# Beacon attention and a maxout FFN in one kernel: pairs 12 and 13 turned by transposing DMAs, and the loop's steps in other places

## The chip, the cores and the metric

The kernel runs on one core of a Trainium2 chip. The metric is the device time of one execution in microseconds; the comparison is between the kernel before and the changed kernel. The core has a matrix engine (PE, with weight loads shown apart as PEld), a vector engine (DVE), a scalar engine (ACT), GpSimd (POOL) and a sync engine (SP), each with its own queue of instructions that run in order. DMA engines move data beside them. PE writes to PSUM, the others read it from there; everything else lives in SBUF.

## The reference

Attention of 64 heads (8 batches of 8) over 576 tokens of width 64, with 16 beacon keys and values per head in front of the causal part; its output, 4608 tokens of width 512, goes through a feed-forward layer with three input matrices and a maximum.

```python
k_all = concatenate([beacon_k, k], axis=2)          # 16 + 576 keys
v_all = concatenate([beacon_v, v], axis=2)
scores = scale * q @ k_all^T                        # beacons seen by all, the rest causal
a = exp(scores - max) / (sum + 1e-09)
x = (a @ v_all) -> (4608, 512)
h = maximum(maximum(x @ w1, x @ w2), x @ w3)        # 512 -> 768
out = h @ w_out                                     # 768 -> 512, float32
```

## The kernel before

**Pairs.** Two heads of a batch are a pair; there are 32 pairs, four to a batch, and two pairs are a quad. For each pair q and k are needed with the 64 columns of both heads on 128 partitions (qT and kT, six buffers of each, used by pair number modulo 6, lines 146 to 152).

**Load, cast, turn.** A pair's q and k come by two loads on SP into a staging tile `st` (eight buffers, `load_pair`, line 192), are cast to bf16 (`cast_piece`, line 252: 96 partitions by 768 elements, one for q and one for k), and are then turned. There are two ways. Pairs below `P_X` are loaded with six neighbouring tokens to a partition (line 202), turned on PE by 12 transposes against the identity (`turn`, line 393, step "pair"), and copied out of PSUM into order by DVE (kT, line 459) and by ACT or DVE (qT, line 448). Pairs from `P_X` on are loaded in token order (line 207) and turned by two transposing DMAs on SP straight from the cast tile into qT and kT (`cross_piece`, line 374, steps "cross" p 0 and "cross" p 1). `P_X` is 14. The 16 beacon columns of kT are copied in by the step "keys" (line 455).

**Scores and masks.** A pair has four groups of score tiles. The step "scores" p g n (line 498) takes a PSUM tile from a ring of three (two named sc, one named wide), puts n spare matmuls of 320 columns on constant data into it (`spare`, line 474), then the scores (line 509), and issues the exponential on ACT (line 524). "score" and "exp" are its two halves apart. "mask" p g engine sets the causal zeros afterwards, on POOL (line 543, affine select) or on DVE (line 541, product with a triangle).

**Values.** When both pairs of a quad are masked, "values" quad half (line 584) multiplies with v (cast by "cast v", line 311) and with ones for the sums; the first half uses the two banks pv0 and pv1, the second a ring tile. "invert" is a logarithm and an exponential on ACT (lines 604 and 606), "multiply" three products on DVE into xT (line 616).

**FFN.** The remaining PE time is filled with units of the feed-forward layer: "ffn 1" with a bank (pv0, pv1, or one half of a ring tile) is one unit, "ffn 2" two units in one ring tile. A unit is four matmuls of 512 columns (line 646), then a cast or a maximum on DVE (lines 654 and 656), or six matmuls (line 682), a copy to y (line 694) and, later, a store (line 720).

**Order.** There is no scheduler: the lists `first_steps` and `loop_steps` are emitted as written, and each engine's queue has its instructions in that order. Where an instruction needs another engine's result it waits, and everything behind it in its queue waits too. "load" n takes the next loads from a fixed list (pairs, v pieces and beacons by batch); with an engine's name, that engine first writes one element of the staging tile, so the engine and not SP waits for the tile to come free. Beside the change stand lines 1034 to 1071 (where pairs 12 to 15 are loaded), and the steps of pairs 8 to 13 (lines 1076 to 1181).

```python
P_X = 14
def cross_piece(p, i):
    src = stage.pop(("pair16", p, i))
    x0 = i * Nb
    nc.sync.dma_start_transpose(
        out=(qTs, kTs)[i][p % NT][:, x0 : x0 + S].rearrange("d (r p) -> d r p", r=QR),
        in_=src.rearrange("p r h d -> p (r h d)"),
    )
```

Of the kernel before, what the change touches and what calls it, by code (L numbers as in the profile page):

```python
# [16 lines left out]
def kernel(  # L17
# [48 lines left out]
    P_X = 14  # L66
# [92 lines left out]
    ring = [(sc_psum, "sc"), (sc_psum, "sc")]  # L159
# [684 lines left out]
    def start_late():  # L844
# [231 lines left out]
        ("scores", 8, 1, 0),  # L1076
# [5 lines left out]
        ("values", 3, 1, "ring"),  # L1082
        ("mask", 8, 1, "pool"),
        ("mask", 8, 0, "pool"),
        ("mask", 8, 2, "pool"),
        ("multiply",),
# [8 lines left out]
        ("scores", 8, 3, 0),  # L1095
        ("scores", 9, 0, 0),
        ("scores", 9, 1, 0),
        ("mask", 8, 3, "pool"),
        ("mask", 9, 0, "pool"),
        ("mask", 9, 1, "pool"),  # L1100
        ("ffn 1", "pv1"),
# [20 lines left out]
        ("ffn 1", "pv1"),  # L1122
# [4 lines left out]
        ("invert",),  # L1127
        ("exp", 10, 2),
        ("values", 4, 1, "ring"),
        ("mask", 10, 1, "pool"),  # L1130
        ("mask", 10, 0, "pool"),
# [4 lines left out]
        ("ffn 2",),  # L1136
        ("ffn 1", "pv0"),
        ("cast", 12, "pool", "pool"),
        ("load", 1),
        ("cast", 14, "pool", "pool"),  # L1140
        ("load", 1),
# [4 lines left out]
        ("mask", 10, 3, "pool"),  # L1146
        ("mask", 11, 0, "pool"),
# [5 lines left out]
        ("cast", 15, "pool", "pool"),  # L1153
        ("load", 1),
# [5 lines left out]
        ("load", 1),  # L1160
# [5 lines left out]
        ("pair", 13, "act"),  # L1166
        ("keys", 13, "act"),
# [7 lines left out]
        ("values", 5, 0, "pv"),  # L1175
        ("invert",),
        ("exp", 12, 2),
# [3 lines left out]
        ("mask", 12, 2, "pool"),  # L1181
        ("multiply",),
        ("invert",),
        ("multiply",),
        ("ffn 2",),
        ("ffn 1", "pv0"),
# [6 lines left out]
        ("keys", 14, "act"),  # L1193
# [4 lines left out]
        ("cross", 16, 0),  # L1198
        ("cross", 16, 1),
        ("cast", 17, "pool", "pool"),  # L1200
        ("cast v", 3, 0),
        ("scores", 13, 2, 0),
        ("scores", 13, 3, 0),
        ("mask", 13, 2, "pool"),
        ("keys", 15, "act"),
        ("mask", 13, 3, "pool"),
        ("ffn 1", "pv0"),
        ("ffn 1", "pv1"),
        ("ffn 1", "pv0"),
        ("cross", 17, 0),  # L1210
        ("cross", 17, 1),
# [5 lines left out]
        ("values", 6, 0, "pv"),  # L1217
        ("invert",),
        ("exp", 14, 2),
        ("values", 6, 1, "ring"),  # L1220
        ("mask", 14, 1, "pool"),
        ("mask", 14, 0, "pool"),
        ("mask", 14, 2, "pool"),
# [3 lines left out]
        ("load", 1),  # L1227
# [3 lines left out]
        ("cast", 18, "pool", "pool"),  # L1231
        ("ffn 1", "pv1"),
        ("scores", 14, 3, 0),
        ("scores", 15, 0, 0),
        ("scores", 15, 1, 0),
        ("mask", 14, 3, "pool"),
        ("keys", 16, "act"),
        ("mask", 15, 0, "pool"),
        ("mask", 15, 1, "pool"),
        ("ffn 1", "pv0"),  # L1240
        ("cross", 18, 0),
        ("load", 1),
        ("cross", 18, 1),
        ("load", 1),
        ("cast", 19, "pool", "pool"),
# [3 lines left out]
        ("mask", 15, 2, "pool"),  # L1249
        ("keys", 17, "act"),  # L1250
# [3 lines left out]
        ("cross", 19, 1),  # L1254
        ("ffn 1", "pv1"),
        ("load", 1),
# [8 lines left out]
        ("mask", 16, 0, "pool"),  # L1265
# [5 lines left out]
        ("cast", 20, "pool", "pool"),  # L1271
# [3 lines left out]
        ("load", 1),  # L1275
        ("scores", 16, 3, 0),
        ("scores", 17, 0, 0),
        ("scores", 17, 1, 0),
        ("mask", 16, 3, "pool"),
        ("keys", 18, "act"),  # L1280
        ("mask", 17, 0, "pool"),
        ("mask", 17, 1, "pool"),
        ("ffn 1", "pv1"),
        ("ffn 1", "pv0"),
        ("cross", 20, 0),
        ("cross", 20, 1),
        ("load", 1),
# [3 lines left out]
        ("cast v", 4, 0),  # L1291
# [12 lines left out]
        ("score", 18, 2),  # L1304
        ("values", 8, 0, "pv"),
        ("invert",),
        ("exp", 18, 2),
        ("values", 8, 1, "ring"),
        ("mask", 18, 1, "pool"),
        ("mask", 18, 0, "pool"),  # L1310
        ("mask", 18, 2, "pool"),
        ("load", 1),
        ("multiply",),
        ("invert",),
        ("multiply",),
        ("ffn 2",),
        ("ffn 2",),
        ("ffn 1", "pv0"),
        ("cast", 22, "pool", "pool"),
        ("ffn 1", "pv1"),  # L1320
        ("scores", 18, 3, 0),
        ("scores", 19, 0, 0),
        ("scores", 19, 1, 0),
        ("mask", 18, 3, "pool"),
        ("keys", 20, "act"),
# [6 lines left out]
        ("cast", 23, "pool", "pool"),  # L1332
        ("store", 1),
        ("load", 1),
# [9 lines left out]
        ("cross", 23, 0),  # L1344
# [3 lines left out]
        ("load", 1),  # L1348
# [6 lines left out]
        ("mask", 20, 1, "pool"),  # L1355
        ("mask", 20, 0, "pool"),
# [5 lines left out]
        ("cast", 24, "pool", "pool"),  # L1362
# [307 lines left out]
```

## Time and profile before

| | us |
|---|---|
| median of 3 runs | 289.59 |
| lowest, highest | 288.01, 289.97 |
| the profiled execution: its own time | 290.2 |
| the profiled execution: span from first to last instruction | 288.4 |
| casts of pairs on POOL, 48 of them, mean | 0.825 |
| transposing DMAs of q, of k: median to landing | 5.1, 3.8 |

The profile is of one execution. Its page gives each engine's busy time, the same in 40 slices of the span with the granted PE clock, the chain of work that ended last, and groups of instructions by source line (L646 is line 646). A timeline row has start, duration, engine, line, operation, output and inputs, the count, and in brackets the idle time before it and what ended that. A windows row has the stretch, its length, and the busy time of PE, PEld, DVE, ACT and POOL with the count of instructions, then PE's clock, the DMA engines' share and GB/s. The loop's steps begin at about 55 us.

### The profile page before, as it was taken

To read this page: it belongs to the slowest core of one execution; us is meant where nothing else is said; L and a number is where in the kernel's file an instruction comes from. 1 tells how busy PE (TensorE), PEld (TensorE's weight loads), DVE (VectorE), ACT (ScalarE), POOL (GpSimd) and SP (SyncE) were. 2 spreads that over 40 slices of the span, in tenths; PEclk is the share of its full clock that TensorE was granted. 3 is DMA by queue.
4 is the path that set the end of the run, shared out by engine and by line. 5 is a ranking of instruction groups with operands and counts; after the bars stand their busy time and mean duration, and the time that the engine had idled before them with its cause. 6 is when DMAs were issued, how large, how long until landed. Compare 5 with 4: busy or idle time off the path is not lost.

```text
span 288.4 us, 8814 instructions
## 1 busy us (share of the span) xinstructions
PE 279.4 (97%) x3702; PEld 160.2 (56%) x3727; DVE 169.6 (59%) x317; ACT 143.9 (50%) x242; POOL 121.6 (42%) x252
## 2 busy tenths in 40 slices
PE   8999999999999999999999999999999999999994
PEld 6666777654645454545456787445544545444442
DVE  2446788756575657464755764666466555373372
ACT  3776676834656564835483268434852552201200
POOL 4463227736486483738366446564623230000000
PEclk9999999999999999999999999999999999999999
DMA  8999999999999979999999999999793003002103
GB/s 155 145 178 202 218 246 168 236 215 205 198 165 160 188 109 127 202 164 194 164 239 192 194 168 213 204 159 181 194 298 152 2 2 148 0 0 102 46 0 147
DMA packets 118231, 45.30 MB, mean 157 GB/s; under 512 B 107312, under 2 KB 112944, under 8 KB 118192
## 3 DMA queue, kind: packets, MB, share of 16 engines
q1 hardware_dynamic: 111984, 39.20, 76.2%
q0 software_dynamic: 5648, 5.21, 12.0%
q8 instruction: 29, 0.48, 0.7%
q10 hardware_dynamic: 560, 0.33, 0.4%
q14 instruction: 10, 0.08, 0.1%
HBM read 35.13 MB, written 9.44 MB: 155 GB/s over the span
## 4 chain that ended last, share of the span: by engine, by line
PE 89%; ACT 3%; DMA 2%; DVE 2%; POOL 1%; issue 1%; POOLq 0%; ACTq 0%
PE pv L646 21%; PE sc L646 15%; PE wide L646 8%; PE pv L682 6%; PE sc L509 6%; PE sc L682 5%; PE pv L584 4%; PE wide L682 4%; PE wide L584 4%; PE sc L584 4%; DMA quad<-in_k_dram 2%; PE wide L509 2%; PE pv L473 2%; ACT at_sb L524 2%; PE sc L665 1%; PE pv L665 1%
## 5 line engine op out<-in xcount | busy, mean ns | idle before, releaser
L524 ACT ACTIVATE at_sb<-sc 128x736 bf16<-128x736 f32 (+5 forms) x95 | 79.4, 868 | 59.6 <-PE sc L509 58.9
L543 POOL TENSOR_SCALAR_AFFINE_SELECT at_sb<-at_sb 128x256 bf16<-128x256 bf16 (+2 forms) x143 | 52.4, 385 | 110.0 <-ACT at_sb L524 101.2
L646 PEld LDWEIGHTS <-w_sb 128*128 128x128 bf16 x648 | 61.1, 98 | 60.7 <-issue 4.9
L646 PE MATMUL pv<-xT,w_sb 128*128 128x512 bf16 (+1 forms) x315 | 65.3, 347 | 0.3
L646 PE MATMUL sc<-xT,w_sb 128*128 128x512 bf16 (+1 forms) x205 | 45.6, 363 | 0.7 <-issue 0.2
L656 DVE TENSOR_TENSOR hT<-hT,pv 128x512 bf16<-128x512 bf16 x48 | 32.4, 686 | 13.2 <-PE pv L646 13.2
L524 ACT ACTIVATE at_sb<-wide 128x736 bf16<-128x736 f32 (+3 forms) x33 | 27.7, 840 | 23.5 <-PE wide L509 23.3
L255 POOL CAST p<-st 96x768 bf16<-96x768 f32 x48 | 38.2, 825 | 0.0
L682 PEld LDWEIGHTS <-hT 128*128 128x128 bf16 x210 | 19.6, 98 | 23.5 <-issue 1.1
L616 DVE TENSOR_TENSOR xT<-pv,recip 128x288 bf16<-128x288 f32 (+2 forms) x48 | 14.2, 351 | 27.1 <-ACT recip L606 27.0
L509 PE MATMUL sc<-qT,kT 64*128 64x288 bf16 (+6 forms) x298 | 28.0, 277 | 1.4 <-DVE kT L443 0.7
L656 DVE TENSOR_TENSOR hT<-hT,sc 128x1024 bf16<-128x1024 bf16 (+1 forms) x19 | 20.8, 1104 | 12.7 <-PE sc L646 12.5
L584 PEld LDWEIGHTS <-v_sb 128*32 128x32 bf16 (+1 forms) x1408 | 24.8, 96 | 2.7 <-issue 1.5
L509 PEld LDWEIGHTS <-kT 64*128 64x128 bf16 x400 | 14.6, 94 | 20.7 <-issue 12.9
L646 PE MATMUL wide<-xT,w_sb 128*128 128x512 bf16 (+1 forms) x110 | 24.5, 364 | 0.1
L682 PE MATMUL pv<-w_out_sb,hT 128*128 128x512 bf16 x83 | 19.9, 380 | 0.1
L311 POOL CAST v_sb<-st 128x1536 bf16<-128x1536 f32 (+2 forms) x21 | 18.4, 898 | 0.0
L654 DVE CAST hT<-pv 128x512 bf16<-128x512 f32 x20 | 13.7, 688 | 5.0 <-PE pv L646 5.0
L682 PE MATMUL sc<-w_out_sb,hT 128*128 128x512 bf16 x68 | 16.4, 380 | 0.2
L665 PEld LDWEIGHTS <-w_sb 128*128 128x128 bf16 x144 | 13.1, 98 | 3.2 <-issue 1.4
L606 ACT ACTIVATE recip<-lnd 128x288 f32<-128x288 f32 x32 | 14.2, 443 | 1.0
L694 DVE COPY y<-pv 128x512 f32<-128x512 f32 x14 | 9.7, 692 | 8.4 <-PE pv L682 8.1
(119 smaller groups left out, 279.8 us busy)
## 6 DMA issues: line engine op xcount, KB each, us to landing
st<-in_q_dram SPq DMA_DIRECT2D x24, 288.0 KB, 5.8
st<-in_k_dram SPq DMA_DIRECT2D x24, 288.0 KB, 6.4
st<-in_v_dram SPq DMA_DIRECT2D x24, 256.0 KB, 5.4
out_dram<-y SPq DMA_DIRECT2D x9, 512.0 KB, 4.6
out_dram<-y SPq DMA_DIRECT2D x17, 256.0 KB, 4.5
w_sb<-in_moe_w_dram POOLq DMA_DIRECT2D x6, 384.0 KB, 8.3
st<-in_v_dram SPq DMA_DIRECT2D x8, 224.0 KB, 4.9
st<-in_v_dram SPq DMA_DIRECT2D x8, 160.0 KB, 5.0
```

The costliest lines, as they stand in the source:

```text
L255: cast(t16.rearrange("p r h d -> p h r d"), st[0:QP, i * NQ2 : (i + 1) * NQ2].rearrange("p (h r d) -> p h r d", h=2, r=QR),)
L311: cast(v_sb[0:n, t:t1].rearrange("p t h d -> p (t h d)"), st[0:n, (t - t_lo) * H * D : (t1 - t_lo) * H * D],)
L509: nc.tensor.matmul(ps[:, e, off : off + q1 - q0], kT[hs, 128 * t : 128 * t + 128], qT[hs, q0:q1], start=True, stop=True, tile_position=(64 ...
L524: nc.scalar.activation(out=both_heads(p, gi), in_=ps[:, :, 0 : g_width(p, gi)], func=AF.Exp, scale=scale)
L543: nc.gpsimd.affine_select(out=view, in_=view, compare_op=ALU.is_ge, fill=0.0, base=x0, pattern=[[0, 2], [1, hi - lo]], channel_multiplier=-1,)
L584: nc.tensor.matmul(ps[bank][32 * j : 32 * j + 32, lo + q0 - qa : lo + qb - qa], lhsT, at_view(PPQ * quad + j // 2, t, j % 2, q0, qb), star ...
L606: nc.scalar.activation(out=recip, in_=lnd, func=AF.Exp, scale=-1.0)
L616: nc.vector.tensor_mul(xT[:, 2 * g + part - 1, c0 + ca : c0 + cb], ps[bank][:, lo : lo + cb - ca], recip[:, ca:cb],)
L646: nc.tensor.matmul(dst[:, o0 : o0 + n], w_in[i][:, ct, 128 * (ft + f) : 128 * (ft + f + 1)], xT[:, ct, x0 : x0 + n], start=(ct == 0), stop ...
L656: nc.vector.tensor_max(h, h, ps)
L665: nc.tensor.matmul(ps[:, f], w_in[i][:, ct, 128 * (ft + f) : 128 * (ft + f + 1)], xT[:, ct, tb * TOKB + lo : tb * TOKB + hi], start=(ct == 0),
L682: nc.tensor.matmul(ps[:, t - tt] if two else ps, hT[:, ft, 128 * t : 128 * (t + 1)], w_out_sb[:, ft, :], start=(ft == 0), stop=(ft == n_ft ...
```

## The change

`P_X` becomes 12: pairs 12 and 13 too are loaded in token order, and their turns on PE ("pair" 12 and 13) are replaced by "cross" 12 and 13. With that the loop's steps are in other places:

- Casts 12 and 13 stand ahead of cast 11; "cross" 12 behind the loads of v for batch 3 and of the beacons, "cross" 13 behind loads 16 and 17.
- Ten spare matmuls are added: scores(8,1) 2, scores(9,0) 2, scores(8,3) 6.
- Some masks go from POOL to DVE, some casts from POOL to DVE (q of 20, 23, 24, 28, k of 31) or ACT (k of 18), some "keys" from ACT to DVE or POOL.
- Several loads get a gate on DVE or POOL, and several loads, crosses and stores move by a few steps.
- In two places an "ffn 2" becomes two "ffn 1" on half ring tiles.

The first steps are the same in both. The diff, cut to what the text below speaks of:

```diff
-    P_X = 14
+    P_X = 12
...
-        ("scores", 8, 1, 0),
+        ("scores", 8, 1, 2),
         ("scores", 8, 0, 0),
...
-        ("cast", 10, "pool", "pool"),
+        ("cast", 10, "pool", "pool"),
+        ("ffn 2",),
+        ("ffn 1", "pv0"),
+        ("load", 1),
+        ("cast", 12, "pool", "pool"),
+        ("load", 1),
+        ("ffn 1", "pv1"),
+        ("ffn 1", "pv0"),
+        ("scores", 9, 0, 2),
         ("scores", 9, 1, 0),
+        ("scores", 8, 3, 6),
+        ("load", 1),
         ("mask", 8, 3, "pool"),
+        ("mask", 9, 1, "dve"),
+        ("ffn 1", "pv1"),
         ("mask", 9, 0, "pool"),
+        ("ffn 1", "pv0"),
+        ("cross", 12, 0),
+        ("cross", 12, 1),
+        ("cast", 13, "pool", "pool"),
+        ("load", 1),
         ("pair", 10, "act"),
-        ("keys", 10, "act"),
+        ("keys", 10, "dve"),
         ("ffn 1", "pv1"),
         ("cast", 11, "pool", "pool"),
-        ("load", 1),
+        ("load", 1, "pool"),
+        ("ffn 2",),
         ("cast v", 2, 0),
...
         ("ffn 1", "pv1"),
+        ("cross", 13, 0),
         ("pair", 11, "act"),
         ("keys", 11, "act"),
         ("ffn 1", "pv0"),
+        ("ffn 1", "pv1"),
+        ("cross", 13, 1),
         ("cast v", 2, 1),
...
-        ("cast", 12, "pool", "pool"),
-        ("load", 1),
         ("cast", 14, "pool", "pool"),
...
-        ("pair", 12, "act"),
-        ("keys", 12, "act"),
...
-        ("cast", 13, "pool", "pool"),
-        ("load", 1),
...
-        ("pair", 13, "act"),
-        ("keys", 13, "act"),
...
         ("score", 14, 2),
         ("values", 6, 0, "pv"),
-        ("invert",),
         ("exp", 14, 2),
+        ("invert",),
...
-        ("cast", 18, "pool", "pool"),
+        ("cast", 18, "pool", "act"),
...
         ("ffn 2",),
-        ("cast", 20, "pool", "pool"),
+        ("load", 1),
+        ("cast", 20, "dve", "pool"),
         ("ffn 1", "pv0"),
         ("ffn 1", "pv1"),
         ("ffn 1", "pv0"),
...
         ("scores", 17, 2, 0),
         ("scores", 17, 3, 0),
-        ("mask", 17, 2, "pool"),
-        ("keys", 19, "act"),
+        ("mask", 17, 2, "dve"),
+        ("keys", 19, "dve"),
+        ("ffn 1", "pv0"),
         ("mask", 17, 3, "pool"),
-        ("ffn 1", "pv0"),
         ("ffn 1", "pv1"),
-        ("cross", 21, 0),
-        ("cross", 21, 1),
         ("cast v", 4, 1),
         ("scores", 18, 1, 0),
...
-        ("cast", 23, "pool", "pool"),
+        ("cast", 23, "dve", "pool"),
...
         ("ffn 1", "pv0"),
+        ("mask", 19, 3, "dve"),
         ("keys", 21, "act"),
-        ("mask", 19, 3, "pool"),
-        ("ffn 1", "pv0"),
         ("ffn 1", "pv1"),
...
-        ("ffn 2",),
+        ("ffn 1", "ring"),
+        ("ffn 1", "ring"),
...
         ("ffn 1", "pv1"),
-        ("ffn 2",),
-        ("store", 1),
+        ("ffn 1", "ring"),
+        ("store", 1),
+        ("ffn 1", "ring"),
         ("store", 1),
```

More of the change, by code (lines that the diff above doesn't have):

```diff
@@ L1146 @@
         ("mask", 10, 3, "pool"),
+        ("cast", 15, "pool", "pool"),
+        ("keys", 12, "act"),
         ("mask", 11, 0, "pool"),
@@ L1180 @@
         ("mask", 12, 0, "pool"),
[L1181 removed]
+        ("keys", 15, "act"),
+        ("exp", 12, 2),
         ("multiply",),
+        ("mask", 12, 2, "dve"),
         ("invert",),
@@ L1198 @@
         ("cross", 16, 0),
+        ("load", 1, "pool"),
         ("cross", 16, 1),
+        ("scores", 13, 3, 0),
         ("cast", 17, "pool", "pool"),
@@ L1254 @@
         ("cross", 19, 1),
+        ("mask", 15, 2, "pool"),
         ("ffn 1", "pv1"),
-        ("load", 1),
         ("scores", 16, 1, 0),
@@ L1285 @@
         ("cross", 20, 0),
-        ("cross", 20, 1),
-        ("load", 1),
+        ("cast v", 4, 0),
         ("cast", 21, "pool", "pool"),
@@ L1315 @@
         ("multiply",),
+        ("load", 1),
         ("ffn 2",),
         ("ffn 2",),
+        ("cast", 22, "pool", "pool"),
         ("ffn 1", "pv0"),
-        ("cast", 22, "pool", "pool"),
         ("ffn 1", "pv1"),
         ("scores", 18, 3, 0),
+        ("scores", 19, 1, 0),
+        ("mask", 18, 3, "dve"),
         ("scores", 19, 0, 0),
-        ("scores", 19, 1, 0),
-        ("mask", 18, 3, "pool"),
-        ("keys", 20, "act"),
+        ("cross", 21, 0),
+        ("cast", 23, "dve", "pool"),
         ("mask", 19, 0, "pool"),
@@ L1361 @@
         ("ffn 2",),
-        ("cast", 24, "pool", "pool"),
+        ("mask", 20, 1, "pool"),
+        ("cast", 24, "dve", "pool"),
         ("ffn 1", "pv0"),
         ("scores", 20, 3, 0),
+        ("load", 1, "dve"),
         ("scores", 21, 0, 0),
@@ L1382 @@
         ("scores", 21, 2, 0),
+        ("cross", 24, 1),
         ("scores", 21, 3, 0),
-        ("mask", 21, 2, "pool"),
-        ("keys", 23, "act"),
         ("mask", 21, 3, "pool"),
+        ("keys", 23, "pool"),
+        ("cast", 25, "pool", "pool"),
         ("ffn 1", "pv0"),
```

183 lines of the change are left out of this document (83 added, 100 removed).

## The prediction

> **What bounds the kernel now.** I read the page first: busy times, clock, chain; then the waits of PE, the windows, and the timeline around the steps that move.
>
> ```profile
> span 288.4 us, 8814 instructions
> ...
> PE 279.4 (97%) x3702; PEld 160.2 (56%) x3727; DVE 169.6 (59%) x317; ACT 143.9 (50%) x242; POOL 121.6 (42%) x252
> ...
> PEclk9999999999999999999999999999999999999999
> ...
> PE 89%; ACT 3%; DMA 2%; DVE 2%; POOL 1%; issue 1%; POOLq 0%; ACTq 0%
> ```
> PE works 97% of the span at full clock, and 89% of the chain that ended last is PE. So a change can gain only by taking work off PE or by closing one of PE's holes. From the view of PE's waits (total, times, longest), of the windows, and of the timeline:
>
> ```profile
> PE pv L584 <- issue: 0.7, 1, 0.7
> ```
> ```profile
> 64.00:72.00 8.00, 7.95 (x56) 3.65 (x55) 5.27 (x8) 3.14 (x6) 4.38 (x7) 1.00 1.26 212
> ```
> ```profile
> 57.84 0.47 PE L584 MATMUL pv<-at_sb,v_sb 128*32 128x176 bf16 x23 [0.73 <-issue]
> ```
> This is the only wait of PE over 0.2 us behind the first steps: a hole of 0.73 us, at 57.1 to 57.8, that no other engine or DMA ends. The window at 64, where the change begins to bite, is full (second column: PE 7.95 of 8), and so are those behind it. There is almost no waiting for other orders of the steps to remove; there is waiting that they could add.
>
> **The change, part by part.**
>
> *The two turns leave PE.* Pairs 12 and 13 each lose 12 transposes. Pair 12's turn in the timeline, and what follows it:
>
> ```profile
> 84.05 0.68 PE L393 MATMUL wide<-ident,p 96*128 96x96 bf16 x12
> 84.56 1.89 PE L646 MATMUL sc<-xT,w_sb 128*128 128x512 bf16 x8
> ```
> From start to next start 0.51, and pair 13's is of the same form: -1.02 us on the path. Their copies out of PSUM leave DVE and ACT, which are not on the path: nothing. No rival "it does not do so" is needed: the built order has 48 transposes at this line instead of 72.
>
> *Ten spare matmuls come onto PE*: two in scores(8,1), two in scores(9,0), six in scores(8,3). The nearest row is a run of seven of the same width:
>
> ```profile
> 24.99 1.12 PE L473 MATMUL sc<-busy 128*128 128x320 bf16 x7
> 26.05 0.49 PE L509 MATMUL sc<-qT,kT 64*128 64x288 bf16 x8
> ```
> 1.06 us for seven, 0.15 each. Eight of them stand where PE has no hole: +1.21. The first two stand just ahead of the hole at 57.1; between 0 (swallowed) and +0.30, I take +0.15.
>
> *Loads 12 and 13 in token order* go from runs of 1536 B to runs of 256 B, in a stretch where DMA is full (share 1.26 in the window above). The k loads of 12, 13 (L202) and of 14, 15 (L207, already in the new form): issues (start, us), then, in the same order, the DMA view's times from issue to landing (last column):
>
> ```profile
> 61.28 0.45 SPq L202 DMA_DIRECT2D st<-in_k_dram  x1
> ...
> 62.27 0.45 SPq L202 DMA_DIRECT2D st<-in_k_dram  x1
> ...
> 63.26 1.07 SPq L207 DMA_DIRECT2D st<-in_k_dram  x1
> ...
> 69.05 1.53 SPq L207 DMA_DIRECT2D st<-in_k_dram  x1
> ```
> ```profile
> st<-in_k_dram SPq DMA_DIRECT2D x1, 288.0 KB, 5.9
> ...
> st<-in_k_dram SPq DMA_DIRECT2D x1, 288.0 KB, 7.0
> ...
> st<-in_k_dram SPq DMA_DIRECT2D x1, 288.0 KB, 9.2
> ...
> st<-in_k_dram SPq DMA_DIRECT2D x1, 288.0 KB, 6.6
> ```
> They land at 67.2, 69.3, 72.5 and 75.7: two loads per step, so 1.05 us a load in the old form and 1.6 in the new. Hence k12 at about 68.3, k13 at 71.5, and everything behind them in the queue some 2.2 us later.
>
> *Casts 12 and 13 move ahead of cast 11 on POOL* (before, they came behind it). Queued behind them now: masks 8,3 and 9,0, cast 11, cast v(2,0), masks 9,2 and 9,3, cast v(2,1); PE waits for cast 11 (turn of pair 11) and for the rest (values 4).
>
> ```profile
> L255 POOL CAST p<-st 96x768 bf16<-96x768 f32 x48 | 38.2, 825 | 0.0
> ...
> L543 POOL TENSOR_SCALAR_AFFINE_SELECT at_sb<-at_sb 128x256 bf16<-128x256 bf16 x84 | 33.9, 409 | 80.5 <-ACT at_sb L524 71.7 <-issue 7.9 <-DMA st<-in_v_dram 0.9
> ```
> ```profile
> 73.67 0.68 PE L393 MATMUL wide<-ident,p 96*128 96x96 bf16 x12
> ...
> 76.67 0.40 PE L584 MATMUL pv<-at_sb,ones 128*32 128x288 bf16 x12
> ```
> k12 cast by 69.1; three mask pieces, 1.2, to 70.3; q13 to 71.2; k13, landed at 71.5, to 72.3; cast 11, 1.65, to 74.0. PE comes to that turn at 73.67 + 1.36 to 1.5 (the spares) = 75.0 to 75.2: 1 us of slack, so 0. v(2,0) and v(2,1), five pieces of 512 columns a row, take 2.7 by the cast's rate, the two masks between them 0.8: 77.5, against values 4 at 76.67 + 1.4 = 78.1: 0. Without the spares the slack would be gone.
>
> *Four transposing DMAs on SP.* Those of 12 stand behind the beacon loads, ahead of load 16; those of 13 behind loads 16 and 17. The nearest rows are pair 14's, and where PE first needs pairs 12 and 13:
>
> ```profile
> 80.55 0.38 SPq L207 DMA_DIRECT2D st<-in_q_dram  x1
> ...
> 87.24 3.23 SPq L374 DMA_TRANSPOSE qT<-p  x1
> ...
> 90.58 1.20 SPq L374 DMA_TRANSPOSE kT<-p  x1
> ```
> ```profile
> qT<-p SPq DMA_TRANSPOSE x18, 5.1
> kT<-p SPq DMA_TRANSPOSE x18, 3.8
> ```
> ```profile
> 90.94 0.33 PE L509 MATMUL sc<-qT,kT 64*128 64x288 bf16 x4
> ...
> 98.32 0.53 PE L509 MATMUL sc<-qT,kT 64*128 64x336 bf16 x6
> ```
> SP reaches load 16 at 80.55; 2.2 later is 82.8. Two issues of 1.2 to 3.2 and 3.8 to land: pair 12 is there at 89 to 93, most likely 89, since little else is then under way. PE wants it at 90.94 + 0.3 (1.36 more, 1.02 less) = 91.2: cost 0, or 2 at the bad end. Pair 13 goes out some 6 us later, 95 to 99 against 98.6. Loads 16 to 18 and pair 14's transposes go back by 3 to 6 us, and their readers stand a block of two pairs or more behind: 0.
>
> A rule speaks against this part: the Trainium skill, "VectorE: DVE Perf Modes", section "The three transpose paths", advises TensorE for a full transpose wherever PSUM is an acceptable destination (390 ns against 1309 ns by DMA per 128x128). At that price, an estimate, a pair's nine tiles would take 11.8 us, and pair 12 would come at 94.6, 3.4 after PE wants it, which would give 293.7. The rows above, both transposes of a pair within some 5 us, do not bear that out here.
>
> *Masks, casts and keys on other engines.* The built order gives DVE 25 more mask pieces, 5 casts, 4 key copies and 7 gate memsets. Where DVE has time this costs nothing; what counts is a place where PE wants a PSUM bank next. Most of the masks stand beside the values (DVE then waits for recip). Two places do not. First, cast 20 between two copies of y:
>
> ```profile
> 123.59 1.23 DVE L694 COPY y<-wide 128x1024 f32<-128x1024 f32 x1 [0.35 <-PE wide L682]
> ...
> 125.98 1.03 PE L646 MATMUL pv<-xT,w_sb 128*128 128x512 bf16 x4
> ```
> ```profile
> L227 DVE CAST h<-h 96x384 bf16<-96x384 f32 x2 | 0.6, 352 | 3.7 <-DMA h<-in_k_dram 3.7
> ```
> The first copy ends at 124.82; plus a cast of 0.35 to 0.70 (once to twice the half-width row; I take 0.6), plus the y copy of the pv bank, as wide as the hT evacuations below, 0.69: 126.1, against 125.98: +0.1. Second, mask 17,2 and keys 19, ahead of the last two evacuations before values 8:
>
> ```profile
> 132.39 0.94 ACT L524 ACTIVATE at_sb<-sc 128x928 bf16<-128x928 f32 x1 [2.71 <-PE sc L509]
> ...
> 134.37 0.69 DVE L656 TENSOR_TENSOR hT<-hT,pv 128x512 bf16<-128x512 bf16 x1 [0.17 <-PE pv L646]
> ...
> 134.93 0.31 PE L584 MATMUL pv<-at_sb,ones 128*32 128x288 bf16 x4
> ```
> The exponential ends at 133.33; mask and copy, about 0.5, 133.85; two evacuations, 135.25; values 8 wants its second bank some 0.2 after 134.93: +0.1. Mask 19,3 stands likewise before values 9: +0.1. I add 0.1 for the four single ring units that replace two double ones (two evacuations of 0.69 for one of 1.23). Sum of these: +0.4, from 0 to 0.8.
>
> *Gates and later transposes.* The gated loads wait on casts a block or more old; the transposes of 20, 21 and 23 that move back still stand well ahead of their scores: 0. The exponentials put ahead of the inversions (14, 18) hold the products back by one exponential, 0.94, under two double ring units of PE work, each longer than that: 0.
>
> **Sum**: -1.02 + 1.21 + 0.15 + 0.4 = +0.7 us. Against its own execution (290.2 us, span 288.4) that is 290.9. The median of the three runs, 289.59, lies 0.6 below it, so I predict 290.3.
>
> **The rivals.**
> *Slower: the cast chain.* Place: the turn of pair 11. It decides once k12 lands after 69.4, and then costs one for one. The longest landing of a k load in this profile:
>
> ```profile
> st<-in_k_dram SPq DMA_DIRECT2D x1, 288.0 KB, 10.0
> ```
> With that, k12 lands at 71.3, 3.0 late, of which 2.0 come through: 292.3, and 293.5 with another 1.2. For it: the full DMA. Against it: 5.9 where it stands now. 0.13.
>
> *DVE stands behind POOL.*
>
> ```profile
> 32.73 0.29 DVE L541 TENSOR_TENSOR at_sb<-at_sb,tri 128x256 bf16<-128x256 bf16 x1
> ...
> 51.34 1.61 POOL L255 CAST p<-st 96x768 bf16<-96x768 f32 x2
> ...
> 52.22 0.86 DVE L541 TENSOR_TENSOR at_sb<-at_sb,tri 128x256 bf16<-128x256 bf16 x1
> ```
> The same mask takes 0.29 alone and 0.86 when it starts under a POOL cast, and ends just after that cast. If the moved masks and casts meet casts like this where DVE has no slack, each costs up to 0.83: three places, values 8 and 9 and cast 20, make +2.5 at most: 291 to 292.8. 0.15. The Trainium skill, "SBUF — State Buffer", section "Who interferes with whom", says that of a GpSimd instruction that reads SBUF and a VectorE one with two SBUF inputs the second one blocks fully. By that rule every meeting costs the rest of the POOL instruction; the trace agrees (0.86 above). Against the price: at most of these places POOL has finished.
>
> *The transposes come late.* Place: the first scores of pair 12, which wait once its k lands after 91.2, one for one. At the bad end above, 93, they wait 2: 292.3. For it: the issue of 3.23 and the queue's 2.2 us; against it: little else is under way then. 0.03.
>
> *Better: the hole closes.* If the 0.73 at 57.1 is a matter of where PE's instructions lie, it may go with four new rows ahead of it, and the first two spares hide in it: -1.02 + 1.21 + 0.4 - 0.73 = -0.1, so 289.5; with no DVE delays 289.0. 0.12.
>
> **Numbers.** My forecast has 0.57 (289.6 to 291.2), the rivals 0.13, 0.15, 0.03 and 0.12. About 1% (2.9 us) is what a measurement of this kernel can tell from no change. Faster by that means below 286.7: no hole is that large, 0.04. Slower means above 292.5: half of the first rival, a third of the second, part of the late transposes, and something unseen, 0.18 together. The same: 0.78. Range 288.5 to 292.8.
>
> **What would show it.** L393 with 48 transposes; L473 with 71 matmuls; PE at the turn of pair 11 without a wait; the first scores of pair 12 without a wait for DMA; L541 on DVE near 0.3 a piece. I am wrong if a window of PE between 60 and 100 falls below 7.5 of 8, if PEclk falls, or if L541's mean exceeds 0.5.

## The result, and the profile after

The changed kernel takes 293.37 us in the median of five runs, against 289.59 for the kernel before: a ratio of 1.0115 (95% interval 1.0081 to 1.0149). The ratio leaves out the slowest of the five, 295.58, in which PE's granted clock was lower (0.994). Measured once more with the experiments, it took 292.67, ratio 1.0087 (1.0062 to 1.0113). The prediction was 290.3, range 288.5 to 292.8. The change costs some 3 us where 0.7 were expected.

The profiled execution took 294.19 us. From its page, and from the view of PE's waits (total, times, longest):

```profile
span 292.3 us, 8830 instructions
...
PE 280.3 (96%) x3687; PEld 159.8 (55%) x3713; DVE 176.2 (60%) x358; ACT 142.9 (49%) x233; POOL 108.9 (37%) x230
...
PEclk9999999999999999999999999999999999999999
...
PE 78%; DMA 6%; POOL 4%; issue 3%; SPq 3%; DVE 2%; ACT 2%; POOLq 0%; DVEq 0%; ACTq 0%
```
```profile
PE sc L509 <- DVE y L694: 1.8, 1, 1.8
PE pv L584 <- issue: 1.3, 1, 1.3
```
PE's busy time (279.4 and 280.3 us) and clock are nearly as before; its share of the chain fell from 89% to 78%, and those of DMA, POOL and SP grew. Scores waiting for DVE's copy of y (L694) are new: no such wait stood in the profile before. The windows say where: first the kernel before, then the changed one.

```profile
184.00:192.00 8.00, 7.95 (x46) 3.53 (x44) 4.96 (x6) 2.94 (x5) 4.38 (x7) 1.00 1.16 189
```
```profile
184.00:192.00 8.00, 6.23 (x37) 2.70 (x36) 3.04 (x7) 2.51 (x4) 1.60 (x4) 1.00 0.98 247
```
All windows from 64 to 184 are full (7.89 to 8.00). The hole lies 90 us behind the steps of pairs 12 and 13. The timeline there, of the kernel before and then of the changed one (SPq L720 is the issue of a store of y):

```profile
175.64 1.67 SPq L720 DMA_DIRECT2D out_dram<-y  x2
```
```profile
182.65 1.23 DVE L694 COPY y<-sc 128x1024 f32<-128x1024 f32 x1 [0.35 <-PE sc L682]
```
```profile
182.38 2.02 SPq L720 DMA_DIRECT2D out_dram<-y  x2
...
186.34 1.23 DVE L694 COPY y<-sc 128x1024 f32<-128x1024 f32 x1 [2.46 <-DMA out_dram<-y]
...
187.62 0.34 PE L509 MATMUL sc<-qT,kT 64*128 64x288 bf16 x4 [1.77 <-DVE y L694]
```
The copies of y use nine buffers in turn (line 846), so the copy at 186.34 needs the one that was written some 95 us earlier, and its store had only just gone out. The DMA view gives 3.9 us from issue to landing for this store: 182.38 + 3.9 = 186.3, which is when the copy starts. In the kernel before the same store took 4.5 and landed at 175.64 + 4.5 = 180.1, 2.5 us ahead of its copy. It is now issued 6.7 us later and lands 6.2 later, and PE was 1.2 us behind by then (the copy would have started at 183.88): 6.2 - 2.5 - 1.2 = 2.5, and DVE stood 2.46. Behind the copy wait the ring tile, the next scores, and PE. Two more copies, at 158.16 and 191.65, wait 2.48 and 2.63 us for their stores in the same way; PE shows no wait of 0.1 us or more for these.

A second, smaller loss follows, by the same lateness:

```profile
194.19 1.76 POOL L255 CAST p<-st 96x768 bf16<-96x768 f32 x2 [4.93 <-DVE hT L654]
...
197.47 0.86 PE L584 MATMUL pv<-at_sb,ones 128*32 128x288 bf16 x12
```
POOL stands 4.93 us for a cast of pair 29, whose load SP had issued at 187.77 and 188.22. DVE's hT, which the row names, has nothing to do with it: the cast reads the staging tile only, the transposes that free its output went out at 178.87 and 181.10, and the first of the two loads took 6.3 us to land, to 194.1. The masks of quad 12 stand behind that cast, and the values take 0.86 us for a run that takes 0.41 elsewhere.

### The profile page after: what moved, and what is told of

Its sections match the earlier page's. It is cut to its first block, busy times and chain, and to the rows that moved or that the text cites. A ratio compares the mean times of both kernels' runs of the same rounds, so it can differ in the third digit from the quotient of the medians.

```text
span 292.3 us, 8830 instructions
## 1 busy us (share of the span) xinstructions
PE 280.3 (96%) x3687; PEld 159.8 (55%) x3713; DVE 176.2 (60%) x358; ACT 142.9 (49%) x233; POOL 108.9 (37%) x230
## 4 chain that ended last, share of the span: by engine, by line
PE 78%; DMA 6%; POOL 4%; issue 3%; SPq 3%; DVE 2%; ACT 2%; POOLq 0%; DVEq 0%; ACTq 0%
PE pv L646 17%; PE sc L646 14%; PE wide L646 7%; PE sc L682 6%; PE pv L682 5%; PE sc L509 5%; PE sc L584 4%; PE pv L584 3%; DMA w_sb<-in_moe_w_dram 3%; PE wide L682 3%; PE wide L584 3%; DMA st<-in_k_dram 2%; PE wide L509 2%; PE pv L473 2%; POOL p L255 2%
## 5 line engine op out<-in xcount | busy, mean ns | idle before, releaser
L524 ACT ACTIVATE at_sb<-sc 128x992 bf16<-128x992 f32 (+5 forms) x93 | 77.4, 856 | 57.6 <-PE sc L509 54.7
L543 POOL TENSOR_SCALAR_AFFINE_SELECT at_sb<-at_sb 128x256 bf16<-128x256 bf16 (+3 forms) x118 | 43.1, 385 | 110.8 <-ACT at_sb L524 95.5
L524 ACT ACTIVATE at_sb<-wide 128x736 bf16<-128x736 f32 (+3 forms) x35 | 30.6, 875 | 31.7 <-PE wide L509 30.9
L646 PE MATMUL sc<-xT,w_sb 128*128 128x512 bf16 (+1 forms) x191 | 43.8, 370 | 0.4
L255 POOL CAST p<-st 96x768 bf16<-96x768 f32 x42 | 33.7, 825 | 15.1 <-DVE hT L654 4.9
L584 PEld LDWEIGHTS <-v_sb 128*32 128x32 bf16 (+1 forms) x1408 | 24.8, 96 | 3.2 <-issue 2.1
L646 PE MATMUL wide<-xT,w_sb 128*128 128x512 bf16 (+1 forms) x125 | 26.4, 352 | 0.2
L656 DVE TENSOR_TENSOR hT<-hT,sc 128x1024 bf16<-128x1024 bf16 (+1 forms) x17 | 18.4, 1093 | 13.2 <-PE sc L646 12.7
L541 DVE TENSOR_TENSOR at_sb<-at_sb,tri 128x256 bf16<-128x256 bf16 (+4 forms) x46 | 12.5, 300 | 18.3 <-ACT at_sb L524 16.3
L682 PE MATMUL sc<-w_out_sb,hT 128*128 128x512 bf16 x85 | 20.5, 380 | 0.3
L694 DVE COPY y<-pv 128x512 f32<-128x512 f32 x14 | 9.6, 689 | 9.4 <-DMA out_dram<-y 5.4
```

The lines of the kernel that those rows point to most:

```text
L255: cast(t16.rearrange("p r h d -> p h r d"), st[0:QP, i * NQ2 : (i + 1) * NQ2].rearrange("p (h r d) -> p h r d", h=2, r=QR),)
L524: nc.scalar.activation(out=both_heads(p, gi), in_=ps[:, :, 0 : g_width(p, gi)], func=AF.Exp, scale=scale)
L543: nc.gpsimd.affine_select(out=view, in_=view, compare_op=ALU.is_ge, fill=0.0, base=x0, pattern=[[0, 2], [1, hi - lo]], channel_multiplier=-1,)
L584: nc.tensor.matmul(ps[bank][32 * j : 32 * j + 32, lo + q0 - qa : lo + qb - qa], lhsT, at_view(PPQ * quad + j // 2, t, j % 2, q0, qb), star ...
L646: nc.tensor.matmul(dst[:, o0 : o0 + n], w_in[i][:, ct, 128 * (ft + f) : 128 * (ft + f + 1)], xT[:, ct, x0 : x0 + n], start=(ct == 0), stop ...
L656: nc.vector.tensor_max(h, h, ps)
```

## Where the time went, step by step

Each kernel runs the same 16 "values" steps on PE. The start of each (the first row of L584 with ones) is a clock that all traces share. Lag behind the kernel before, us:

| values at (before) | 32.65 | 56.26 | 118.5 | 147.9 | 177.56 | 193.99 | 206.96 |
|---|---|---|---|---|---|---|---|
| changed kernel | -0.35 | +0.43 | +0.97 | +1.00 | +1.48 | +3.48 | +3.95 |
| changed kernel, again | +0.04 | +0.37 | +1.01 | +1.15 | +2.89 | +3.86 | +4.29 |
| three stores moved up | -0.30 | +0.24 | -0.32 | -0.32 | +0.14 | +0.14 | +0.14 |
| six stores moved up | -0.59 | +0.53 | +0.68 | +0.69 | +1.25 | +1.25 | +2.70 |
| changed up to cross 17 only | -0.37 | +0.58 | +0.72 | +0.72 | +2.75 | +4.32 | +4.33 |
| the same without the four transposes | +0.45 | +0.79 | +0.19 | +0.18 | +0.18 | +0.17 | +0.18 |
| changed behind cross 17 only | +0.15 | +0.16 | -0.49 | -0.48 | +0.43 | +1.67 | +1.67 |
| the same without gates | -0.68 | -0.69 | -0.56 | -0.56 | -0.57 | -0.57 | -0.56 |

The first column lies in steps that are the same in all; it shows how far one execution differs from another, by up to 1 us. Read differences along a row. From 147.9 to 206.96 the changed kernel loses 2.95 (again: 3.14). That is the larger part of the change's cost; the rows before 147.9 add 1.35 (again: 1.11), of which the last sections tell.

## The experiments

PE's total wait for copies of y is given as "PE for y", and SP's first store of each group of three as "stores".

**Three stores up.** The stores behind cross 26 and 27 go ahead of cross 25, nothing else:

```diff
+        ("store", 1),
+        ("store", 1),
+        ("store", 1),
         ("cross", 25, 0),
...
         ("cross", 26, 1),
-        ("store", 1),
         ("ffn 1", "pv1"),
-        ("store", 1),
...
         ("cross", 27, 1),
-        ("store", 1),
```


> The changed kernel with one thing moved: the three stores that stand behind cross 26 and cross 27 on SP are issued ahead of cross 25. Theory (SP is late): DVE's copy of y waits because the buffer that it writes, one of nine, is still to be stored, and that store stands on SP behind the transposing DMAs of pair 26. Then the copies of y at about 184 to 187 us start without a wait for a DMA, PE's hole of 1.8 us before the scores of pair 24 goes, and the time falls by 1.8 to 2.2 us against the changed kernel, to 291.2 to 291.6. Rival (the store is only the first of several late things): the stores push cross 25 and cross 26 back by some 3 us, and PE waits for these instead; the time stays at 293 or more.

Measured: 291.24, ratio 1.0057 (1.0033 to 1.0082). SP's and DVE's rows:

```profile
169.73 2.51 SPq L720 DMA_DIRECT2D out_dram<-y  x3
```
```profile
182.79 1.23 DVE L694 COPY y<-sc 128x1024 f32<-128x1024 f32 x1 [0.25 <-PE sc L682]
```
The copy no longer waits for a DMA, PE for y is 0, and the lag stays at +0.14 from 177 on; no first scores waited in their place. So the late store is the cause of the hole. The time lies in the theory's range. The fall is less certain: by the ratios it is 1.7 us against the first measurement of the changed kernel and 0.9 against the second, where 1.8 to 2.2 were expected.

**Which half of the change makes SP late?** The order up to cross 17 of one kernel, joined to the order from there on of the other.

> The changed kernel up to cross 17 (pairs 12 and 13 turned by DMA, the ten spares, all moves of steps of pairs 8 to 13), the kernel before from there on. Theory (the four added transposes set SP back by 6 to 7 us, and it never catches up): the stores at 176 us in the kernel before come at about 182 here too, a copy of y waits 2 us or more at 183, and the time is 292 to 293. Rival (the order behind cross 17 sets SP back, by crosses that wait for casts moved behind other work): SP has caught up by 150 us, no copy of y waits before 200 us, and the time is 290.0 to 290.6, the spares and turns alone.

> The kernel before up to cross 17 (P_X 14, no spares), the changed kernel's order from there on. Theory (the added transposes set SP back): SP is on time here, no copy of y waits, and the time is 289.6 to 290.3. Rival (the order behind cross 17 does it): SP is late by 5 us or more at the stores of about 182 us, the copies of y wait, PE has the hole of about 1.8 us, and the time is 292 to 293.

The first took 294.05, ratio 1.0146 (1.0111 to 1.0181); the second 291.23, ratio 1.0041 (1.0017 to 1.0065). PE for y 3.1 and 1.7. Stores at 143.38 and 175.64 in the kernel before; in these two:

```profile
150.68 0.40 SPq L720 DMA_DIRECT2D out_dram<-y  x1
...
181.23 1.71 SPq L720 DMA_DIRECT2D out_dram<-y  x2
```
```profile
148.41 0.40 SPq L720 DMA_DIRECT2D out_dram<-y  x1
...
180.53 1.95 SPq L720 DMA_DIRECT2D out_dram<-y  x2
```
Either half alone is enough to make SP late by some 5 us. Neither theory had that: the first kernel came out as its theory said, though 1 us slower, the second against its theory, nearly as late as its rival said, but faster. In the first kernel SP's instructions behind cross 17 are those of the kernel before, and it is 5.6 us late 60 us on: here the lateness on SP did not go away.

**The first half: transposes or loads?** The first half again, without the transposing DMAs of pairs 12 and 13; and the kernel before with only the loads of 12 and 13 in runs of 256 bytes.

```diff
         x0 = i * Nb
+        if p in (12, 13):
+            return
```
```diff
-            if p < P_X:
+            if p < P_X - 2:
```


> The changed order up to cross 17 (with the spares) and the kernel before from there on, but with the four transposing DMAs of pairs 12 and 13 left out, so that these pairs' scores use what earlier pairs left in the buffers. It stands against the same kernel with them, where the stores came at 150.7 and 181.2 us and PE stood 3.1 us for copies of y. Theory A (the four transposing DMAs set SP back): the stores come at 143 to 146 and 175 to 177 us, no copy of y holds PE, 290.0 to 291.0. Theory B (the loads of 12 and 13 in runs of 256 bytes do, or the places of the loads): the stores stay at 149 us or later, PE stands 2 us or more, 292.5 to 294.

> The kernel before with one thing changed: pairs 12 and 13 are loaded in token order, in runs of 256 bytes, but still turned on PE in the old way, so that their tokens are out of order. Theory A (the transposing DMAs set SP back, the loads do not): stores at 143 to 145 and 175 to 177 us, 289.6 to 290.4. Theory B (the loads do): the stores at 148 us or later and at 179 us or later, copies of y wait, 291.5 or more.

Without the transposes: 290.78, ratio 0.9999 (0.9961 to 1.0036), PE for y 0, and SP in time (line 722 is the store there):

```profile
143.18 0.40 SPq L722 DMA_DIRECT2D out_dram<-y  x1
...
174.81 1.49 SPq L722 DMA_DIRECT2D out_dram<-y  x2
```
The loads alone: 290.20, ratio 0.9993 (0.9967 to 1.0019). Its traced execution took 984.75 us, over three times as long as the nine others, so where its stores stand is not shown. The loads in short runs stand in the kernel without the transposes too, and its stores are in time. Theory A holds: the four transposing DMAs set SP back, the loads do not. In the changed kernel their four rows on SP add up to 6.1 us (1.29, 1.27, 2.28 and 1.28), about what SP is late by.

**The second half: the gates.**

> The kernel before up to cross 17 and the changed order from there on, where SP was late without any added DMA; here without the fourteen gates of that part. With the gates SP stood 5.2 us, to 117.3 us, for one on POOL. Theory (that gate sets SP back, and SP never catches up): the stores come at 143 to 146 and 175 to 178 us, no copy of y holds PE, 289.7 to 290.5. Rival (the order of the crosses behind cross 17 sets SP back in any case): stores at 148 us or later, PE stands 1 us or more, 290.8 to 291.6.

Measured 289.42, ratio 0.9994 (0.9967 to 1.0021), PE for y 0. SP with the gates, the gate on POOL that it waits for, and SP without gates:

```profile
110.81 1.20 SPq L374 DMA_TRANSPOSE qT<-p  x1
117.28 0.33 SPq L207 DMA_DIRECT2D st<-in_q_dram  x1
```
```profile
116.39 0.82 POOL L255 CAST p<-st 96x768 bf16<-96x768 f32 x1
117.15 0.10 POOL L198 MEMSET st<- 96x1 f32 x1
```
```profile
109.80 1.20 SPq L374 DMA_TRANSPOSE qT<-p  x1
111.05 0.58 SPq L207 DMA_DIRECT2D st<-in_q_dram  x1
```
Without gates SP issues the same load at 111.05, so its tile was free by then; the gate opened at 117.2, because it stood in POOL's queue behind four masks, the first of which waited 5.4 us for its exponential, and two casts. Stores came at 144.72 and 174.96 without gates. The theory holds, though the time lies a little under its range.

**Gates off in the changed kernel.**

> The changed kernel with the sixteen gates of the loop taken off: SP itself waits for the staging tile of each load. Theory (a gate on DVE or POOL opens late because it stands behind a mask or behind a copy of y that waits for a store, and holds SP): SP reaches the loads of 118 and 159 us 1 to 5 us sooner, the copies of y wait less, and the time falls by 1 to 2 us against the changed kernel, to 291.3 to 292.4. Rival (SP is late from the added transposes and loads, the gates add nothing): the stores of 182 us come within 1 us of that, and the time stays at 293.0 to 293.7.

Measured 293.36, ratio 1.0123 (1.0084 to 1.0161), stores at 150.39 and 180.64, PE for y 1.2. The time is the rival's, but the stores of 182 us came 1.7 us sooner, which the rival had ruled out, and PE waits less for y, as the theory said. In the changed kernel a gate stood on DVE behind a copy that waited for a store, and SP (free at 157.1) behind the gate; a late store makes SP later still:

```profile
158.16 0.69 DVE L694 COPY y<-pv 128x512 f32<-128x512 f32 x1 [2.48 <-DMA out_dram<-y]
...
158.80 0.06 DVE L198 MEMSET st<- 96x1 f32 x1
```
SP issued that load at 158.91 with the gate and at 157.25 without. What took the gain back, in this one profile, is a wait called issue that the changed kernel has not (0.16 us at most), of the kind explained below:

```profile
171.96 0.26 PE L584 MATMUL sc<-at_sb,v_sb 128*32 128x96 bf16 x5 [1.20 <-issue]
```
The gate of 117 us costs little here: it opens at 118.62, and SP, late from the transposes, is free at 118.37. So the two causes do not add up: the second store is 5.6 us late by the transposes alone, 4.9 by the other half alone, 6.7 by both, 5.0 with the gates off.

**Six stores up, and the spares.** Three more stores go from behind cross 22 and 23 to ahead of cross 22; then also without the ten spares; and the changed kernel without the spares alone.

> The changed kernel with six stores moved on SP: three from behind cross 22 and cross 23 to ahead of cross 22, three from behind cross 26 and cross 27 to ahead of cross 25. Theory (stores that stand too late on SP are all that the copies of y wait for): no copy of y waits for a DMA before 200 us, and the time is that of the kernel with three stores moved or up to 0.5 us less, 290.7 to 291.3; what is left over the kernel before, some 1 us, is PE's own (the spares, single ring units). Rival (the stores ahead of cross 22 set the crosses back): first scores of a pair wait for a DMA, 291.5 or more.

> The same with the ten spare matmuls left out too. Theory (PE's path is full, the spares stand on it): 1.3 us less than with them, 289.4 to 290.0. Rival (the spares cover waits for casts and masks): PE waits at other places, as in the kernel without spares alone, where it idled 0.61 us at 68.5 and 0.77 us at 149.9; the time is 290.4 to 291.0.

> The changed kernel without its ten spare matmuls. Theory (they stand on PE's path, at 0.15 us each): the time falls by 1.2 to 1.5 us, to 291.9 to 292.2, if PE's hole at 57 us stays as it is. Rival (they only fill time in which PE would wait for casts and masks, or the later wait for a store takes the gain back): the time stays at 293.0 to 293.6, and the hole of 1.8 us at 186 grows by as much as the spares gave.

Ratios 1.0068 (1.0041 to 1.0094), 1.0046 (1.0011 to 1.0081) and 1.0064 (1.0036 to 1.0091); medians 291.71, 291.48 and 291.66. With six stores up no copy of y waits for a DMA before 200 us, but the time was no better than with three (1.0068 against 1.0057, each within the other's interval). In its profile POOL's late cast costs instead:

```profile
193.02 1.70 POOL L255 CAST p<-st 96x768 bf16<-96x768 f32 x2 [4.69 <-DMA st<-in_q_dram]
```
```profile
196.54 0.56 PE L584 MATMUL pv<-at_sb,ones 128*32 128x176 bf16 x6 [0.92 <-POOL at_sb L543]
```
All three times miss what was expected: 291.71 lies above the theory's range, 291.48 above both ranges, 291.66 below both. By the ratios, taking the spares out gave the changed kernel 0.7 to 1.5 us, where ten at 0.15 us are 1.5; once six stores are up it gave 0.6 (0.2 by the medians). That kernel's profile has a wait called issue of 1.10 us at 151.8; the one with spares has one of 0.36 at 169.6 in its place.

**The best that could be hoped for, and a control.**

> The changed kernel's order up to cross 17 without the spares, the order of the kernel before from there on, and the six stores moved ahead of cross 22 and cross 25. Theory (the two turns are worth 1.02 us of PE, and only the late stores took it away): 288.6 to 289.2, below the kernel before. Rival (something else behind cross 17 depends on SP being in time, casts or first scores): PE waits there, and the time is 290 or more.

> The kernel before with the same six stores moved ahead of cross 22 and cross 25. Theory (in the kernel before the stores come in time, no copy of y waits before 240 us): no change, 289.3 to 290.1. Rival (moving stores up is a gain or a loss by itself): 1 us or more away from the kernel before. PE's hole at 57 us shows once more how it varies where the steps ahead of it are the same.

The first: 291.17, ratio 1.0056 (1.0030 to 1.0081), where 288.6 to 289.2 was hoped for. PE waits for nothing late any more, and yet it lost. Its profile has two waits called issue that the kernel before has not, 0.31 us at 120.7 and 0.44 at 150.6, and the one near 57 us is 1.64 long. The control: 289.84, ratio 0.9993 (0.9974 to 1.0012); moving stores is neither gain nor loss by itself. The control's wait near 57 us is 0.54. So these waits differ by 1.85 us; from 32.65 to 206.96 the first kernel (lag -0.77 to +0.54) loses 1.51 against the control (-0.20 to -0.40) where 1.02 was to be gained, 2.5 in all, and the waits are the larger part of that.

**The waits called issue.** Number PE's instructions in the order of the program, a matmul and its weight load as two, its few semaphore instructions included. The wait at 57 us then lies, in every kernel that shows it, in front of number 1985, whatever matmul that is. In the kernel without spares the new ones lie in front of numbers 3777 and 4545, that is 1985 + 7 x 256 and 1985 + 10 x 256 (here and below to within one):

```profile
119.70 1.47 PE L682 MATMUL sc<-w_out_sb,hT 128*128 128x512 bf16 x5 [0.21 <-issue]
```
```profile
149.93 0.21 PE L584 MATMUL sc<-at_sb,v_sb 80*32 80x80 bf16 x2 [0.77 <-issue]
```
Two kernels test it: matmuls of 16 columns that shift the numbers, 23 in the kernel that was to be the best, 34 in the kernel before (a negative count stands for these).

```diff
...
-        ("scores", 8, 1, 0),
+        ("scores", 8, 1, -34),
```


> The kernel that has the changed order up to cross 17 without the spares, the order of before from there and the six stores up, with 23 matmuls of 16 columns on constant data put into scores(8,1), so that PE's instructions from there on have the numbers that they have in the kernel before. Theory (the waits of PE called issue, 0.31 us at 120.7 and 0.44 at 150.6 without these, lie where PE comes to every 256th instruction, at 1985 + 256 n, inside a dense run of small matmuls): both are gone, as in the kernel before; PE pays 0.5 to 1.0 us for the 23, and the time is 290.5 to 291.2. Rival (these waits come from something else that the order up to cross 17 has): they stay where they are, and the time is 291.5 to 292.2.

> The kernel before with 34 matmuls of 16 columns on constant data put into scores(8,1): 68 more instructions on PE, nothing else. Theory (as for the 23): new waits called issue, 0.2 to 1.2 us each, at the end of the values steps of about 107, 136, 180 and 209 us, whose dense run now begins 17 to 31 instructions behind the number 1985 + 256 n; together with 0.7 to 1.4 us for the matmuls the time is 291.5 to 293.5. Rival (the place of an instruction does not matter): no new waits, and the time is 290.3 to 291.1, the matmuls alone.

With 23: 291.36, ratio 1.0041 (1.0015 to 1.0067). The waits at 120 and 150 are gone, as the theory said, with the lag at -0.16 from 91 us to the end. The time lies between the two ranges, because one that nobody had foreseen, of 1.22 us, came at 61, in front of number 2241 = 1985 + 256:

```profile
61.06 1.24 PE L682 MATMUL sc<-w_out_sb,hT 128*128 128x512 bf16 x5 [1.22 <-issue]
```
With 34: 293.97, above the theory's range, ratio 1.0118 (1.0084 to 1.0152). New waits in front of 2241, 3521 and 5569, all 1985 + 256 n:

```profile
62.40 0.26 PE L584 MATMUL wide<-at_sb,v_sb 128*32 128x96 bf16 x8 [1.65 <-issue]
```
```profile
111.08 1.25 PE L646 MATMUL sc<-xT,w_sb 128*128 128x512 bf16 x4 [0.39 <-issue]
```
```profile
183.39 0.26 PE L584 MATMUL sc<-at_sb,v_sb 128*32 128x96 bf16 x5 [0.17 <-issue]
```
Of the four places named ahead two came, small ones; the 1.65 at 62.4 came in a place that was not named. The numbers fit in every case; how long a wait is was not foretold.

The traces also hold what ends these waits. The page counts a DMA queue called instruction, and the trace has the time of each of its 29 packets:

| kernel | wait in front of | packet, in order | packet from, to (us) | wait ends | behind the packet |
|---|---|---|---|---|---|
| before | 1985 | 7th | 55.10, 56.39 | 57.84 | 1.45 |
| before, 34 added | 2241 | 8th | 59.46, 60.76 | 62.40 | 1.63 |
| before, 34 added | 3521 | 13th | 108.58, 109.46 | 111.08 | 1.62 |
| changed, without spares | 4545 | 17th | 147.14, 148.49 | 149.93 | 1.44 |

So it is in all 27 such waits of 0.15 us or more behind the first steps, over sixteen traces: the wait in front of 1985 + 256 n ends 1.2 to 1.8 us behind the end of packet 7 + n. PE waits for its own instructions.

**The changed kernel again.**

> The changed kernel once more, unaltered. Theory: the same as before, 1.0115 times the kernel before or up to 1.015; the profile shows the copy of y at about 184 us waiting for a store and PE's hole ahead of the first scores of pair 24. If that hole was an accident of one execution, the profile is without it and the time is within 1.007.

The ratio, 1.0087, lies below the theory's 1.0115 and above the 1.007 of an accident. The copies of y wait again. PE stands 1.21 us at 157.06 and 0.79 at 188.06, together 2.0 against 1.77 at one place: the amount repeats, its place between two groups of copies does not.

## Why the prediction was wrong, by its own steps

*The step that failed* is what the prediction said of what is queued behind on SP: "Loads 16 to 18 and pair 14's transposes go back by 3 to 6 us, and their readers stand a block of two pairs or more behind: 0", and of the gates, "The gated loads wait on casts a block or more old ... : 0". The size was nearly right: loads 16 and 17 were issued 4.2 and 4.4 us later, load 18 9.5, pair 14's transposes 7.4 and 5.9, the store of 143 us 6.4. Wrong was to follow only the readers of the next few loads. SP is one queue to its end, and lateness on it stayed at 5 to 7 us for 100 us. Two readers far behind had less slack than that: the copies of y, by the store that frees their buffer (2.5 us in the kernel before), and POOL's cast of pair 29. The stores were never in the sum. For the gates the tile was indeed free, as the text said; but the engine that opens a gate does so when its own queue comes to it: 6 us later at 117 in the kernel with the second half alone, and 1.7 us later at 158.8 in the changed kernel.

*None of the prediction's signs showed it.* L393 has 48 transposes, L473 71 matmuls, L541 a mean of 0.30, and no window of PE between 64 and 104 falls below 7.89. The signs looked at 60 to 100 us, where the steps move; the loss lies behind 147.9.

*The hole at 57* is a wait at PE's instruction 1985, and the prediction's suspicion, that it is a matter of where PE's instructions lie, was right. It did not close: from nothing to 1.64 us over these profiles, 1.35 and 1.45 in the changed kernel's against 0.73 before. That is 0.6 to 0.7 us of the lag, which the sum did not have.

*Two turns off, spares on* (-1.02 + 1.21): from the start of the loop's first output unit (59.78 before, lag +0.73) to 118.5 (+0.97) the lag grew by 0.24, in two other kernels with the same steps too; +0.19 was said. *The first two spares*, 0.15 of 0 to 0.30: from the values at 47.62 to those at 56.26 the seven kernels with these spares gain 0.34 to 0.35 of lag, the three changed ones without any spare or added matmul 0.00; full price.

*Masks, casts, keys and single ring units*, +0.4: the lag moved by 0.03 from 118.5 to 147.9, where the masks and casts of the sum lie (again: 0.14). The clean case is the kernel with the changed order behind cross 17 and no gates: it has all of these steps, the ring units too, and its lag stays at -0.56 to the end. So this term was nothing. L541 takes the 0.3 us a piece that was expected, so the rival of DVE behind POOL did not happen:

```profile
L541 DVE TENSOR_TENSOR at_sb<-at_sb,tri 128x256 bf16<-128x256 bf16 (+4 forms) x46 | 12.5, 300 | 18.3 <-ACT at_sb L524 16.3 <-ACT kT L455 2.0
```
*Casts 12 and 13 ahead of 11*: cast 11 was to be done at 74.0; POOL's three casts end at 71.60 + 2.37 = 73.97, and the turn of pair 11 starts at 75.70 without a wait:

```profile
71.60 2.37 POOL L255 CAST p<-st 96x768 bf16<-96x768 f32 x3
...
75.70 0.68 PE L393 MATMUL wide<-ident,p 96*128 96x96 bf16 x12
```
*Pair 12's transposes in time*: yes; SP issued them at 82.07 and 83.41, and the first scores of pair 12 show no wait. The Trainium skill, "VectorE: DVE Perf Modes", section "The three transpose paths", gives a transpose by DMA 1.3 us for a tile of 128x128. That price did not show here: each of pair 12's two, four and a half tiles, landed 2.6 us after its issue. The Trainium skill, "VectorE: DVE Perf Modes", section "Rules for kernel authors", advises TensorE where PSUM will do as the destination. No kernel here with the added transposing DMAs was faster than the one with the turns on TensorE, so the advice holds in this case, but for another reason: a transposing DMA occupies SP's queue for 1.2 us and more, a load's issue for 0.3 to 0.6 when nothing holds it.

So PE's own part is about 0.24 + 0.35 + 0.03 = +0.6, where the prediction's terms make +0.74; that these are close is partly luck, since the spares cost 0.2 more and the masks 0.4 less than said. Of the 4.3 us of lag between 32.65 and 206.96, 0.6 is this, 0.6 the hole at 57, and 2.95 SP's lateness, which the sum put at 0.

**What stays open.** Why SP does not catch up: its rows from 100 to 182 us stand end to end, in the kernel before too, yet a good part of that is waiting. Whether the wait at 57 us is longer with the changed order or by chance: kernels with the changed order up to there have 0.20 to 1.64, those with the order of before 0 to 0.86. And some 0.6 us of the kernel with three stores up: its +1.65 over the kernel before (by the ratio) is 0.6 of PE's own, 0.46 between 147.9 and 177.56, where a copy of y still waited 2.5 us, and a rest that its one profile, of an execution of 290.15 us, does not show. No version beat the kernel before; the two full ones that equal it have no added transpose and no added gate.

## What to carry to other kernels

When an in-order queue gets more to do, find the tightest slack of everything behind it to the end of the program, not of the next few readers, and look above all at stores, whose reader is the reuse of a buffer. A gate on another engine opens when that engine's queue gets to it, not when the tile is free. And where PE is full, a gain of a microsecond can be lost by what the edit does to others: the four DMAs that were to save 1.02 us of PE's transposes cost some four by themselves (ratio 1.0146 with them, 0.9999 without, in an otherwise equal kernel).

## What the runs showed of the hardware

*PE's instructions come in blocks of 256.* The waits called issue behind the first steps lie at 1985 + 256 n of PE's instructions, except one of 0.16 us at 243 to 248 us, which five traces have at one and the same FFN step, whatever its number. They come only where a block is used up fast: a values step runs 240 instructions in 2.3 us, a unit of the FFN 8 in 0.9. The page counts the transfers of instructions:

```profile
q8 instruction: 29, 0.48, 0.7%
```
In the trace each of the 29 packets has 16384 bytes, 64 for each of 256 instructions. The Trainium skill, "Runtime: NRT & Kernel Launch", section "Instruction fetch mechanics", says that the instruction memory is refilled in blocks of 16 KiB, 256 instructions, by a DMA queue of its own, and that crossing a block is mostly hidden. The trace agrees on both: behind the first steps at most four crossings of an execution show a wait. But these few cost 0.16 to 1.65 us each. So adding or removing a few small matmuls moves every later boundary, into a values step or out of it, and may cost as much as the edit gains.

*Lateness on SP persisted in this kernel.* The delay of four transposing DMAs issued at 82 to 93 us is still 5.6 us at 181, and that of a stand of 5.2 us at 112 to 117, which adds no transfer at all, is 4.9 at 180.5.
